# A scan and gated feed-forward kernel: its head reordered, small work moved to GpSimd, weight loads moved

## The chip, the cores and the metric

The kernel runs on one core of one Trainium2 chip. The metric is the time of one execution on the device, in microseconds; of the kernel before there are three runs, whose median is compared. A core has TensorE (PE, with PEld for its weight loads), VectorE (DVE), ScalarE (ACT), GpSimd (POOL) and SyncE (SP), which run side by side, each its own instructions in their order, and wait for each other on semaphores. DMA transfers are issued by SP and ScalarE on hardware queues (q1 and q10 in the profile) and by GpSimd on a software queue (q0), and all of them share 16 DMA engines.

## What is computed

A Mamba-2 style scan over 4 batches, 8 heads and 768 tokens, and a bilinear feed-forward layer on its output. Cut to what matters:

```python
for c in range(nc):                          # chunks of tokens
    cum = np.cumsum(log_a[chunk], axis=-1)
    L = np.exp(cum[:, None] - cum[None, :]) * causal
    M = (Cc @ Bc.T) * L                      # scores, masked and decayed
    y[chunk] = M @ xc + (Cc @ state) * np.exp(cum)
    state = np.exp(cum[-1]) * state + (Bc * np.exp(cum[-1] - cum)).T @ xc
x2 = y.transpose(0, 2, 1, 3).reshape(3072, 256)
out = ((x2 @ w_a) * (x2 @ w_b)) @ w_out      # 256 -> 1536 -> 256
```

Inputs and output are float32. The kernel uses blocks of 128 tokens, six in all, and running products of `a` in place of sums of logarithms.

## The kernel before

Tokens go by blocks of 128 (`NBLK` = 6); a block of all four batches is two pairs of two batches each, so pairs 0 and 1 are block 0, pairs 2 and 3 block 1, and so on. All is written for one core under a schedule given by hand: each engine's instructions stand in the order of the code, and the tile framework only adds the waits. Every transfer stands on its issuer's queue in that order too.

*Loads.* SP and ScalarE load `a` and B and C (`bn`, `cn`) of pairs 0 and 1 (lines 192 to 202). GpSimd loads x of pair 0 (`xn`), half 0 of Wa, x of pair 1, half 0 of Wb and half 1 of Wa (227 to 233), all cast to float16 on the way; half 1 of Wb comes later (812), and the two halves of Wo at 870 and 880. SP's loads of C and B of block 1 (`cq`, `bq`, 813) wait until half 0 of Wa has landed, and x and B of pairs 2 and 3 follow them.

*The chain of a pair in block 0.* VectorE scans `a` to running products (`scan`, 242) and takes the reciprocal at mid block (`over_mid`); TensorE turns the two into per-token factors (`factors_mm`, 257). B and C are scaled by them (`scale_bc`, 318, to `bm` and `cm`), transposed on TensorE (`transposes`, 361) and copied out by VectorE (`bt`) and ScalarE (`ct`). `scores` (392) makes C B^T in four PSUM banks, `mask` (436) multiplies by the causal table, three of four times on VectorE, once by a ScalarE copy `tmp` and a product on GpSimd. The output product (`pv_u`, 445, for pair 0; `pv1`, 516, for pair 1) multiplies by x, and the result is copied to `X2T`, the feed-forward layer's input. `ds_mm` makes the state's contribution.

*The feed-forward layer of block 0.* `unit_mm` (588) makes two of twelve slices of 128 of x2 @ w_a or x2 @ w_b in one bank, four matmuls of 256 columns. `evac_a` (605) copies the first factor to SBUF on ScalarE; `times` (610) multiplies by the second on VectorE, or, with `by_pool`, after another ScalarE copy on GpSimd; `go` (728) runs whole units. `out_mm` (629) multiplies by Wo. The four banks for all this and for the factors go round in the order of the digits of `BANKS` (22), one per `bank()` call.

*Later blocks* take their factors from rows (`mid_rows`, 280; `turned_rows`, 290, a transpose on VectorE to `Pt`; `batch_factors`, 295, four copies to `FC`; `batch_inverse`, 302, their reciprocal `FB`). `scale_q` (335) multiplies C and B by them on GpSimd into `planes`, whose gaps `clear` (286) has set to zero, and `turn` (347) transposes them on VectorE. `state_sums`, `state_spread` and `state_decay` (562 to 587) carry the state, with decay tables `G` and `Ge` (862, 864; `Ge` uses `parS`, 824, which is `par` times a constant).

*Fillers.* `warmup` (235) issues matmuls on zeros that nothing reads, in places where TensorE would else have nothing to do.

The step of this schedule that the change touches is lines 769 to 891. After it TensorE runs the blocks 1 to 5 by the same functions.

Of the kernel before, what the change touches and what calls it, by code (L numbers as in the profile page):

```python
# [19 lines left out]
SS = 64.0  # L20

BANKS = (
    "012313123123123012301230120312301223012301203120312032130210321032130123012301203213021302"
    "1301203120312031201320132013201320132013201320312031203120312031203120312031203120312"
# [4 lines left out]
def kernel(  # L29
# [100 lines left out]
    def bank(name):  # L130
        return psf.tile([128, 512], f32, name=name, tag=f"ff{next(banks)}")
# [84 lines left out]
    )  # L216
    by_row = ident[0:BH, 0:BH].rearrange("p (b g e) -> p b g e", b=nb, e=2)
# [14 lines left out]
    load_w(0, Wb)  # L232
# [69 lines left out]
    def batch_inverse(lo, hi):  # L302
        nc.vector.reciprocal(FB[:, lo:hi], FC[:, lo:hi])
# [284 lines left out]
    def unit_mm(p, k2, W):  # L588
        ps = bank("aps" if W is Wa else "bps")
        for kk in range(2):  # L590
# [178 lines left out]
    warmup(6, SC[3])  # L769
    warmup(2, SC[3], 128)  # L770
# [8 lines left out]
    warmup(1, SC[3], 128)  # L779
# [4 lines left out]
    mid_rows(0, 1, nc.vector)  # L784
# [11 lines left out]
    clear(planes[0], nc.vector)  # L796
# [3 lines left out]
    scale_bc(1, 0, nc.gpsimd)  # L800
# [6 lines left out]
    scale_bc(1, 1, nc.vector)  # L807
    pv_u(0, 1, py, True)
    for bt in range(2):
        evac0(1, bt, (nc.scalar, nc.vector)[bt], py)  # L810
    scan(4, 5)
# [11 lines left out]
    turned_rows(0, 1)  # L823
    nc.vector.tensor_scalar(parS, par, SS, None, ALU.mult)
    scan(5, NBLK)
    over_mid(2, NBLK)
    clear(planes[1], nc.vector)
# [15 lines left out]
    mid_rows(1, NT, nc.gpsimd)  # L843
# [3 lines left out]
    warmup(1, fps[:, 128:512], 384)  # L847
    bps = [unit_mm(0, k2, Wb) for k2 in range(2)]
    gps = fps[:, 96 : 96 + H // 2 * NG]
# [10 lines left out]
    times(0, 0, bps[0], asb[0])  # L860
    pv1()
    nc.scalar.copy(G.rearrange("p g k -> p (g k)"), gps)
    batch_factors(0, 1, *range(nb))
# [6 lines left out]
    load_wo(0)  # L870
    ds_mm(0, SC[0][:, 0:256])
    bps.append(unit_mm(0, 2, Wb))
    for k2 in range(1, 3):
        times(0, k2, bps[k2], asb[k2])
    batch_inverse(0, 1)
    nc.vector.reciprocal(flat(fB, 1, 2), fps[:, 2 * NBP * H : 4 * NBP * H])
    scale_q(2, 1, nc.gpsimd)
    scale_q(3, 1, nc.gpsimd)
    scale_q(2, 0, nc.gpsimd)
    load_wo(1)  # L880
    scale_q(3, 0, nc.gpsimd)
    go((1, 0), (1, 1), (1, 2))
    state_sums(0)
# [4 lines left out]
    for (p, k2), a_sb_ in zip(late, asb):  # L888
        times(p, k2, unit_mm(p, k2, Wb), a_sb_)
        if k2 == 3 and p == 0:  # L890
            turn(2)
# [171 lines left out]
```

## Time and profile before

| | |
|---|---|
| median of 3 runs | 123.48 us (123.34 to 124.47) |
| the profiled execution | 123.55 us, span 121.8 us |
| busy: TensorE, VectorE, ScalarE, GpSimd | 116.1, 90.4, 67.2, 56.5 us |
| fillers on TensorE (line 237, by their two outputs and the third) | 23 instructions, the last at 12.86 us |
| B of pair 1, asked for by ScalarE | issued 3.60 us, 6.4 us to landing |
| half 0 of Wa, half 0 of Wb, half 1 of Wa, half 1 of Wb | issued 4.05, 6.12, 6.81, 10.72 us; 5.9, 6.6, 8.9, 7.4 us to landing |
| half 0 and half 1 of Wo | issued 16.04, 21.03 us; 7.1, 5.3 us to landing |
| first product of Wo (line 632) | 24.98 us |

The profile is of one execution, by the hardware's own records. Its page gives busy times, the span in 40 slices, the DMA queues, the chain of work that ended last, and the costliest groups of instructions; the trace behind it answers for single instructions, their waits and their transfers. Busy shares are means over the span, and engines wait for different things at different times, so a stage is read by what its last wait was for.

### The profile page before, as it was taken

To read this page: it belongs to the slowest core of one execution; us is meant where nothing else is said; L and a number is where in the kernel's file an instruction comes from. 1 tells how busy PE (TensorE), PEld (TensorE's weight loads), DVE (VectorE), ACT (ScalarE), POOL (GpSimd) and SP (SyncE) were. 2 spreads that over 40 slices of the span, in tenths; PEclk is the share of its full clock that TensorE was granted. 3 is DMA by queue.
4 is the path that set the end of the run, shared out by engine and by line. 5 is a ranking of instruction groups with operands and counts; after the bars stand their busy time and mean duration, and the time that the engine had idled before them with its cause. 6 is when DMAs were issued, how large, how long until landed. Compare 5 with 4: busy or idle time off the path is not lost.

```text
span 121.8 us, 3560 instructions
## 1 busy us (share of the span) xinstructions
PE 116.1 (95%) x1389; PEld 74.2 (61%) x1389; DVE 90.4 (74%) x170; ACT 67.2 (55%) x135; POOL 56.5 (46%) x87
## 2 busy tenths in 40 slices
PE   5989899999999999999999999999999999999990
PEld 2445789788744468644476464766464684655880
DVE  4898987998998995599966989687799435748000
ACT  0435577557767654567666637545645537565220
POOL 7976757789999839395901995200000000000000
PEclk9999999999999999999999999999999999999999
DMA  2999999995969996999952909312001012010132
GB/s 62 135 179 196 221 226 209 143 201 109 101 82 168 113 151 91 100 178 182 223 25 74 97 1 117 21 43 86 5 0 46 11 50 74 0 43 0 43 102 76
DMA packets 59777, 12.13 MB, mean 100 GB/s; under 512 B 54992, under 2 KB 59728, under 8 KB 59760
## 3 DMA queue, kind: packets, MB, share of 16 engines
q0 software_dynamic: 20256, 3.67, 40.8%
q1 hardware_dynamic: 36976, 7.87, 35.9%
q10 hardware_dynamic: 2528, 0.36, 1.8%
q8 instruction: 11, 0.18, 0.6%
q14 instruction: 6, 0.05, 0.1%
HBM read 12.42 MB, written 3.15 MB: 128 GB/s over the span
## 4 chain that ended last, share of the span: by engine, by line
PE 84%; DMA 5%; DVE 4%; ACTq 2%; issue 1%; POOL 1%; ACT 0%; POOLq 0%; DVEq 0%
PE ops L688 22%; PE aps L662 22%; PE bps L662 21%; DMA bn<-in_B_dram 5%; PE ops L632 4%; PE SC L398 3%; PE aps L593 3%; PE bps L593 3%; ACTq L154 2%; PE SC L467 2%; DVE t L443 1%; PE SC L531 1%; DVE hk L617 1%; PE SC L479 1%; DVE bt L379 1%
## 5 line engine op out<-in xcount | busy, mean ns | idle before, releaser
L607 ACT COPY asb<-aps 128x512 f32<-128x512 f32 x72 | 41.9, 586 | 17.1 <-PE aps L662 13.4
L674 DVE TENSOR_TENSOR hkb<-bps,asb 128x512 f16<-128x512 f32 x60 | 40.3, 686 | 12.0 <-ACT asb L607 10.7
L662 PE MATMUL aps<-XB,Wa 128*128 128x512 f16 x120 | 35.8, 379 | 0.0
L662 PE MATMUL bps<-XB,Wb 128*128 128x512 f16 x120 | 35.7, 379 | 0.0
L688 PE MATMUL ops<-Wo,hkb 128*128 128x256 f16 (+1 forms) x252 | 28.1, 268 | 0.0
L688 PEld LDWEIGHTS <-hkb 128*128 128x128 f16 x252 | 23.0, 98 | 3.8
L662 PEld LDWEIGHTS <-Wb 128*128 128x128 f16 x120 | 12.4, 103 | 13.5
L662 PEld LDWEIGHTS <-Wa 128*128 128x128 f16 x120 | 12.1, 103 | 11.7 <-issue 0.5
L443 DVE TENSOR_TENSOR t<-SC,causal_q 128x512 f16<-128x512 f32 x27 | 17.3, 681 | 2.4 <-PE SC L398 2.4
L700 ACT ACTIVATE osb<-ops 128x256 f32<-128x256 f32 (+1 forms) x20 | 7.6, 378 | 18.4 <-PE ops L688 18.4
L441 POOL TENSOR_TENSOR t<-tmp,causal_q 128x512 f16<-128x512 f32 x5 | 5.8, 1156 | 11.4 <-ACT tmp L440 11.4
L176 POOL DMA_DIRECT2D xn<-in_x_dram x8 | 9.6, 1200 | 0.0
L340 POOL TENSOR_TENSOR planes<-cq,FC 128x256 f16<-128x256 f32 x10 | 7.6, 772 | 2.3 <-DMA x<-in_x_dram 2.2
L617 DVE TENSOR_TENSOR hk<-bps,asb 128x512 f16<-128x512 f32 x12 | 7.8, 671 | 1.1 <-PE bps L593 0.6
L340 POOL TENSOR_TENSOR planes<-bq,FB 128x256 f16<-128x256 f32 x10 | 7.7, 774 | 0.1
L443 DVE TENSOR_TENSOR t<-SC,causal 128x512 f16<-128x512 f32 x11 | 6.9, 671 | 0.5 <-PE SC L398 0.5
L553 ACT ACTIVATE XB<-SC 128x512 f16<-128x512 f32 (+1 forms) x10 | 5.1, 552 | 4.0 <-PE SC L495 2.4
L440 ACT COPY tmp<-SC 128x512 f32<-128x512 f32 x10 | 5.9, 588 | 2.2 <-PE SC L398 1.8
L593 PE MATMUL aps<-X2T,Wa 128*128 128x256 f16 x48 | 6.7, 273 | 0.2 <-DVE hk L617 0.2
L593 PE MATMUL bps<-X2T,Wb 128*128 128x256 f16 x48 | 6.8, 273 | 0.0
L441 POOL TENSOR_TENSOR t<-tmp,causal 128x512 f16<-128x512 f32 x5 | 5.8, 1152 | 2.1 <-ACT tmp L440 1.9
L237 PE MATMUL SC<-warm 128*128 128x512 f16 (+1 forms) x15 | 4.9, 473 | 1.3 <-DVE warm L204 1.3
(102 smaller groups left out, 107.2 us busy)
## 6 DMA issues: line engine op xcount, KB each, us to landing
out_dram<-osb SPq DMA_DIRECT2D x23, 128.0 KB, 1.8
cq<-in_C_dram SPq DMA_DIRECT2D x20, 64.0 KB, 4.2
bq<-in_B_dram SPq DMA_DIRECT2D x20, 64.0 KB, 3.8
bn<-in_B_dram SPq DMA_DIRECT2D x8, 128.0 KB, 4.1
xn<-in_x_dram POOLq DMA_DIRECT2D x8, 128.0 KB, 5.6
Wa<-in_moe_w_a_dram POOLq DMA_DIRECT2D x2, 384.0 KB, 7.4
Wb<-in_moe_w_b_dram POOLq DMA_DIRECT2D x2, 384.0 KB, 7.0
Wo<-in_moe_w_out_dram POOLq DMA_DIRECT2D x2, 384.0 KB, 6.2
```

Of the source, the lines that this page charges most:

```text
L176: eng.dma_start(by_token(pair_in[p][which]).rearrange("p t h n -> p (t h) n"), src.rearrange("t h q n -> q (t h) n"))
L340: eng.tensor_tensor(out=plane[:, c0 : c0 + 4 * step].rearrange("p (j c) s -> p j s c", c=step)[:, :, :, 0:N], in0=by_batch[blk][which][:, ...
L440: nc.scalar.copy(tmp, i_)
L441: nc.gpsimd.tensor_tensor(out=o_, in0=tmp, in1=c_, op=ALU.mult)
L443: nc.vector.tensor_tensor(out=o_, in0=i_, in1=c_, op=ALU.mult)
L593: nc.tensor.matmul(ps[:, kk * 2 * Q : (kk + 1) * 2 * Q], W[k // 6][:, f, k % 6 // 3 * 384 : (k % 6 // 3 + 1) * 384].rearrange("p (c kk) -> ...
L607: (nc.vector.tensor_copy if on_dve else nc.scalar.copy)(asb, a_ps)
L617: eng.tensor_tensor(out=s["hk"][:, 2 * k2 : 2 * k2 + 2, :].rearrange("p k q -> p (k q)"), in0=b_ps, in1=asb, op=ALU.mult)
L662: nc.tensor.matmul(t_, W[k // 6][:, f, k % 6 // 3 * 384 : (k % 6 // 3 + 1) * 384].rearrange("p (c kk) -> p kk c", kk=3)[:, k % 3], XB[:, b ...
L674: return lambda: nc.vector.tensor_tensor(out=s["hk"][:, k], in0=ps[1], in1=asb, op=ALU.mult)
L688: nc.tensor.matmul(o_ps[:, 0:w], hk[:, k, c * Q : (c + 1) * Q], Wo[:, k, cs], start=(k == 0), stop=(k == NK - 1), skip_group_check=True,)
L700: nc.scalar.activation(out=o_sb[:, 0:w], in_=o_ps[:, 0:w], func=AF.Copy, scale=1.0 / (YS * YS))
```

## The change

It rewrites the order of the head and of block 0's feed-forward units. Cut to its core:

```diff
@@ tables, behind the reduction to par
+    nc.vector.tensor_scalar(parS, par, SS, None, ALU.mult)
@@ first loads, by GpSimd
         if p == 0:
             w0 = load_w(0, Wa)
-    load_w(0, Wb)
+            load_w(0, Wb)
     load_w(1, Wa)
@@
-    def unit_mm(p, k2, W):
-        ps = bank("aps" if W is Wa else "bps")
-        for kk in range(2):
+    def unit_mm(p, k2, W, ps=None, kks=(0, 1)):
+        if ps is None:
+            ps = bank("aps" if W is Wa else "bps")
+        for kk in kks:
@@ pair 0
-    warmup(6, SC[3])
-    warmup(2, SC[3], 128)
+    warmup(5, SC[3])
+    warmup(1, SC[3], 128)
...
     warmup(2, SC[3])
-    warmup(1, SC[3], 128)
...
-    mid_rows(0, 1, nc.vector)
+    mid_rows(0, 1, nc.gpsimd)
...
-    clear(planes[0], nc.vector)
+    clear(planes[0], nc.gpsimd)
     warmup(1, tcp)
     factors_mm(1, 2, fps, 1)
     warmup(2, tcp)
-    scale_bc(1, 0, nc.gpsimd)
...
     scale_bc(1, 1, nc.vector)
+    scan(4, 5)
+    scale_bc(1, 0, nc.vector)
+    clear(planes[1], nc.gpsimd)
     pv_u(0, 1, py, True)
     for bt in range(2):
         evac0(1, bt, (nc.scalar, nc.vector)[bt], py)
-    scan(4, 5)
     load_w(1, Wb)
@@ pair 1
     transposes(1, apart=True)
     aps = [unit_mm(0, 0, Wa)]
-    turned_rows(0, 1)
-    nc.vector.tensor_scalar(parS, par, SS, None, ALU.mult)
     scan(5, NBLK)
     over_mid(2, NBLK)
-    clear(planes[1], nc.vector)
     clear(planes[2], nc.gpsimd)
...
     mask(product(1, 3), by_pool=True)
-    mid_rows(1, NT, nc.gpsimd)
     asb.append(evac_a(aps[2]))
     for m in range(3):
         mask(product(1, m))
-    warmup(1, fps[:, 128:512], 384)
     bps = [unit_mm(0, k2, Wb) for k2 in range(2)]
+    bps.append(unit_mm(0, 2, Wb, kks=(0,)))
...
     times(0, 0, bps[0], asb[0])
+    times(0, 1, bps[1], asb[1], by_pool=True)
     pv1()
+    ds_mm(0, SC[0][:, 0:256])
+    unit_mm(0, 2, Wb, bps[2], (1,))
     nc.scalar.copy(G.rearrange("p g k -> p (g k)"), gps)
-    batch_factors(0, 1, *range(nb))
-    nc.gpsimd.tensor_tensor(
-        out=Ge.rearrange("p k (g e) -> p g k e", e=2),
-        in0=G.unsqueeze(3).broadcast_to((128, H // 2, NG, 2)),
-        in1=parS.unsqueeze(1).unsqueeze(1).broadcast_to((128, H // 2, NG, 2)),
-        op=ALU.mult,
-    )
-    load_wo(0)
-    ds_mm(0, SC[0][:, 0:256])
-    bps.append(unit_mm(0, 2, Wb))
-    for k2 in range(1, 3):
-        times(0, k2, bps[k2], asb[k2])
+    times(0, 2, bps[2], asb[2])
+    turned_rows(0, 1)
+    mid_rows(1, NT, nc.gpsimd)
+    batch_factors(0, 1, *range(nb), eng=nc.gpsimd)
+    load_wo(0)
+    go((1, 0))
     batch_inverse(0, 1)
+    go((1, 1))
     nc.vector.reciprocal(flat(fB, 1, 2), fps[:, 2 * NBP * H : 4 * NBP * H])
+    go((1, 2))
     scale_q(2, 1, nc.gpsimd)
     scale_q(3, 1, nc.gpsimd)
     scale_q(2, 0, nc.gpsimd)
     load_wo(1)
     scale_q(3, 0, nc.gpsimd)
-    go((1, 0), (1, 1), (1, 2))
     state_sums(0)
+    nc.gpsimd.tensor_tensor(
+        out=Ge.rearrange("p k (g e) -> p g k e", e=2),
+        in0=G.unsqueeze(3).broadcast_to((128, H // 2, NG, 2)),
+        in1=parS.unsqueeze(1).unsqueeze(1).broadcast_to((128, H // 2, NG, 2)),
+        op=ALU.mult,
+    )
     spread(0)
...
-        if k2 == 3 and p == 0:
+        if k2 == 4:
             turn(2)
```

The digits of `BANKS` change with it, so the feed-forward units of the whole kernel go round the four banks in another order. In the new order the bank of Wb unit (1, 1), which `times` on VectorE frees, is the one that Wa unit (0, 3) takes; before, it took that of Wa unit (1, 1), which ScalarE's copy frees. The instructions that compute are otherwise the same: TensorE has one product of 512, two of 128 and one of 384 columns less, all of them fillers, and ScalarE copies one bank more for GpSimd in place of four small copies.

## The prediction

> **What bounds the kernel now.** I read the page's slices first, to see which engine is full and when, then the chain of waits from the start to 16 us, then TensorE's timeline for its own waits, then busy time by stretch, and last the DMA queues around the end of the chain's long transfer.
>
> The slices (tenths of each fortieth of the span, 3.05 us):
> ```profile
> PE   5989899999999999999999999999999999999990
> ```
> TensorE is full from the fifth slice to the end. Only the head, some 15 us, holds time that a new order can give back. The chain of waits (start us, us, what) says what paces it:
> ```profile
> 3.60 6.44 DMA bn<-in_B_dram
> ...
> 10.16 0.63 POOL bm L327
> ...
> 10.84 0.41 PE SC L368 x4
> ...
> 11.27 0.69 DVE bt L379
> 11.96 0.31 DVE Pt L291
> 12.27 0.05 DVE parS L824
> 12.32 0.34 DVE Pr L244
> ...
> 12.82 0.17 DVE planes L288
> 12.99 1.75 DVE t L443 x3
> ```
> B of pair 1, asked for at 3.60, lands at 10.04; call L = 10.07 the moment it counts. From there GpSimd scales it, TensorE transposes, VectorE copies out, then does five small things (transpose, parS, scan, reciprocal, clear) and the masks, and only then can the output product of pair 1 (L452) start, at 14.78, L + 4.71. What TensorE does meanwhile, from its timeline:
> ```profile
> 12.86 0.33 PE L237 MATMUL fps<-warm 128*128 128x384 f16 x1
> 14.78 0.42 PE L452 MATMUL SC<-t,xn 64*32 64x128 f16 x32 [0.40 <-DVE t L443]
> 22.54 0.60 PE L593 MATMUL aps<-X2T,Wa 128*128 128x256 f16 x4 [0.17 <-DVE hk L617]
> ```
> One filler product and one wait of 0.40, then a wait of 0.17 at 22.54, the last in the span that the waits list gives TensorE. By stretch (us; busy PE, PEld, DVE, ACT, POOL; clock; DMA):
> ```profile
> 10.07:14.78 4.71, 4.17 (x76) 2.98 (x62) 4.20 (x12) 2.77 (x6) 3.23 (x8) 1.00 1.19 216
> 14.78:22.50 7.72, 7.60 (x124) 6.80 (x124) 6.64 (x14) 5.04 (x13) 5.39 (x10) 1.00 1.23 207
> ```
> VectorE leaves 0.5 of 4.71 and 1.08 of 7.72 idle. After 22.5 the chain holds TensorE's work alone, which the change keeps, so the end moves by what TensorE has gained when it reaches the scores of pair 2 (23.1).
>
> **The sum's base.** The profiled execution took 123.55, of which 121.8 is the span and 1.75 lies around it; the median of three is 123.48, 0.07 less.
>
> **Scaling B of pair 1 on VectorE.** Before: 0.09 issue + 0.63 on GpSimd + 0.05 = L + 0.77 for the transposes. VectorE did the same shape for pair 0 in 0.42 (L327), so L + 0.56. VectorE must be free at L. It ended pair 0's masks at 9.55; ahead of B now stand cm (0.36) and a scan (0.41), which alone would end at 10.32. But mid_rows (0.27) leaves VectorE ahead of pair 0's bt, which followed it without idle time, and clear (0.17) leaves too; fewer fillers ahead of the first factors let these start when selr is done (3.85) and not at 4.15. Some 0.25 to 0.5 earlier: free at 9.8 to 10.05. If neither reaches the masks, 0.25 of the gain is lost.
>
> **X2T behind it.** The copy-out of output 0's last quarter (0.29) now stands behind bm: done at L + 0.77, so the first Wa products start at L + 0.83 (before L + 1.00); eight take 0.97, and the scores start at L + 1.80 (before L + 1.97).
>
> **The small steps taken out.** Pair 0 shows 7.09 to 7.66 from scores to masks, 0.57. So masks at L + 2.37, if VectorE is free: bt starts 0.43 after the transposes (10.84 to 11.27), L + 0.99, ends L + 1.68, scan 0.34 and reciprocal with its gaps 0.16 end L + 2.18. Before, masks stood at L + 2.92. They end at L + 4.12. The fourth mask is GpSimd's: ScalarE's ct (0.39), two copies (1.07), tmp (0.60) and gaps end about L + 3.1, plus 1.14 is L + 4.25, which is later and decides: the product's second part starts 0.46 earlier than L + 4.71. TensorE's list fits: from L + 2.2 one Wa unit 0.44, ten Wb products 1.1, the G product 0.39 end at L + 4.1; the filler (0.33) is gone. Half of the third Wb unit, two of four products, 0.22, now lies ahead of the output product: that is 0.22 less behind it. So far 0.68.
>
> **Edits that other work hides.** parS (0.12) goes into VectorE's wait of 0.77 for the first transfer; without that cover it would delay the first scan by as much. mid_rows of block 1 (by its row of 512 columns, 1.03, about 0.3) goes into GpSimd's wait of 0.82 ahead of its first mask, two clears (0.23 each) into the wait of 0.62 that bm leaves with it; what is queued behind them, the issue of Wb's second half, still comes sooner than at 10.72, and the planes they clear are first written at 18.96. Uncovered they would cost 0.8 in all. SP's queue keeps its order: C of block 1 waits for the first Wa, as before. turned_rows (0.39) moves behind the masks, into VectorE's wait between two bilinear products.
>
> **GpSimd's new work.** One product of the bilinear stage goes over ScalarE (0.58) to GpSimd (its masks, same size, take 1.15), which frees VectorE of 0.64. GpSimd then does this product (to L + 5.4), mid_rows (1.03, L + 6.45) and four FC copies of 32x32. No row has them there: ScalarE does one in 0.216, GpSimd one three times as wide in 0.259, a memset of one column in 0.10; between 0.10 and 0.26 I take 0.2, nearest to the copies. They end at L + 7.25. The reciprocal FB (0.34) waits for them, with a bilinear product (0.63) queued behind it on VectorE, and that product frees the bank of Wa unit (0,3): L + 8.3. TensorE would reach it at L + 4.25 + 4.10 - 0.22 = L + 8.13 (4.10 from 14.78 to 18.88). A new wait of 0.2, between none and 0.4 with the copies' ends. The wait of 0.17 at 22.54 goes, as VectorE has 0.64 less and turn(2) stands one product later; GpSimd's scale_q for it waits for C of block 1 at 18.96, as before, and ends near 21.2, when VectorE still has products to do. Sum: 0.68 - 0.2 + 0.17 = 0.65.
>
> **Wb ahead of x of pair 1.** Wb lands at 6.12 + 6.6 = 12.7, and its first product is at 13.02; with TensorE earlier it would be the next to be late, so its move is needed and otherwise worth nothing. x of pair 1 (landing 10.2 to 11.4) then comes behind 384 KB, 1.9 us at 207 GB/s: 13.3, still ahead of L + 4.16 = 14.2. What it may cost is L itself. Two answers of the DMA view, 7.5 to 9.0 and 9.0 to 9.5:
> ```profile
> q0 software_dynamic: 244, 0.29, 111.7%
> q10 hardware_dynamic: 66, 0.01, 5.8%
> ...
> q0 software_dynamic: 416, 0.08, 188.7%
> q10 hardware_dynamic: 21, 0.00, 4.6%
> ```
> q10 carries B of pair 1. It passed 44 packets/us beside Wa and 42/us beside x: what q0 moves seemed not to matter, cost zero. From the other side: q0's packets took 0.036 us each while they were x (554 in 9.5 to 10.1 at 209.8% of 16 engines) and 0.111 each while mostly weights (464 in 10.1 to 12.8 at 119.5%). If each of the last 21 packets of B lets one of q0 past, Wb adds 0.075 for each that shares an engine: 0.3 over five engines, 1.6 on one. No gain: the swap changes only what follows Wa on q0. I take 0.1, near the measured rates. The Trainium skill, in DMA: Bandwidth & Descriptors, Queues, rings and completion order, says that each DMA engine goes round its queues a packet at a time; it speaks against this move, and by it the sum would be 0.35 rather than 0.55; the two rates above don't bear it out.
>
> **Wo later.** It was issued at 16.04 and landed at 23.1, used at 24.98. GpSimd now comes to it at about 17.3: landing between 23.1 (if the queue is its limit; Wb's second half lands only at 18.1) and 24.4. It is used at 24.4. Taken as nothing; at worst it eats 0.3. What it leaves free on the engines may bring C of block 1 sooner, which nothing waits for but GpSimd. The later Ge and scale_q keep their cover: spair is read at 29.03.
>
> Forecast: 0.65 - 0.1 = 0.55 gained, 123.55 - 0.55 - 0.07, some 122.95, say 123.0.
>
> **Rivals.** *The gain is given back* on new waits: FB 0.4 for 0.2, Wo 0.3, or B 0.3: 0.55 - 0.2 - 0.3 is about nothing, 123.2 to 123.7. For it: VectorE is busy 6.64 of 7.72 there, and four separate links must each hold. Against: it loses 0.64. *B pushed back, slower*: all the late packets share one or two engines; 1.6 or 0.8 later, less 0.65, is 123.6 to 124.5; it decides from 0.65 on. For it: q10 had passed 406 packets in the microsecond from 6.5, before Wa filled q0, and then 44/us, so q0 paces it. *The clock rises late, slower*: the fillers of 512 columns take 606 to 634 ns until 5.5 and 379 to 390 from 6.1 on, though the clock row shows full throughout. Now TensorE, out of fillers, idles some 0.3 before the first factors. If the rise came after L, the 22 Wa and Wb products ahead of pair 1's output would take some 0.1 more each, 1.3 to 2.2, net 0.7 to 1.6: 124.2 to 125.1. Against: 0.46 of idle time at 6.6 did not undo it. The Trainium skill, in TensorE: Matmul & The Clock Gate, Part 1, has the clock doubled after one busy window of about 3.4 us; that the trace agrees (1.26 to 6.1 busy) is all that it shows, not how much idling a window stands. *More than forecast*: no new wait and all of TensorE's idle time and filler back (0.54 + 0.12 + 0.33 + 0.22): 122.3.
>
> **How the numbers follow.** Forecast 0.48 (122.6 to 123.2), given back 0.27, B pushed back 0.09, late clock 0.07, more 0.09. The range 122.4 to 124.0 leaves out the low half of the last and the high parts of the slower two, about 0.15. One per cent (1.23 us) is what a measurement tells from no change: faster than 122.25 needs the best case and some luck, 0.06; over 124.7, the high ends of B and clock, 0.08; the rest 0.86.
>
> **What would show it.** bm on VectorE within 0.1 of B's landing, B landing before 10.2; L452 starting 0.4 to 0.5 earlier; no filler and no wait over 0.15 before it; FB waiting for GpSimd's FC; scores of pair 2 near 22.5; fillers at 380 ns by 6.5. Wrong if B lands after 10.7, if L632 waits for Wo, or if TensorE waits over 0.5 in all between 15 and 25.

## The result and the profile after

The changed kernel takes 125.14 us (median of 14 runs, 124.05 to 125.82), the kernel before 123.54 (14 runs, 123.34 to 125.36): a ratio of 1.0119, 95% interval [1.0091, 1.0147]. It is 1.6 us slower, where 0.5 faster was forecast. Disturbed runs are left out of the ratios, which are not the quotients of these medians. The profiled execution of the changed kernel took 124.05, with a span of 122.3; it is the fastest of the 14. So there are two things to explain: why even this one is 0.5 behind the profiled execution of before (123.55), and why most executions are a further microsecond behind it.

TensorE's row of the page's slices is as full as before from the seventh slice on (the sixth, 15.3 to 18.3 us, has an 8 for a 9), and tells little:
```profile
PE   5999889999999999999999999999999999999990
```
The chain of waits of the changed kernel (start us, us, what), from the transposes of pair 1 to Wa unit (0, 3) and the two behind it:
```profile
10.52 0.28 PE SC L369 x4
10.80 0.87 PE aps L595 x8
11.67 0.36 PE SC L399 x32
...
14.11 0.42 PE SC L453 x32
14.53 0.32 PE SC L507 x27
14.84 0.92 issue
15.76 0.23 PE SC L507 x4
15.99 0.35 PE bps L595 x2
16.43 0.69 DVE hk L619
17.12 0.31 DVE Pt L292
...
18.21 0.21 POOL FC L298
...
18.72 0.64 DVE hk L619
19.40 1.47 PE aps L595 x12
```
The first four lines are the head as forecast. B and GpSimd have left the chain, and TensorE is its own limit up to the output product of pair 1 (L453), which starts at 14.11 and not at 14.78: 0.67 earlier. Then comes a stretch that the kernel before did not have, 0.92 of "issue", a wait for nothing that the profile shows: of the 32 products of L507, 16 of `ds_mm(1)` in `pv1` and then 16 of `ds_mm(0)`, 28 are done, and the last four start only at 15.76. From there the chain goes through VectorE and GpSimd and back to TensorE at 19.40.

TensorE's timeline gives its waits (start us, us, engine, line, operation, in brackets the idle time ahead and what ended it):
```profile
3.90 0.61 PE L266 MATMUL fps<-selr,Pr 32*64 32x16 f32 x8 [0.21 <-DVE selr L251]
15.76 0.23 PE L507 MATMUL SC<-xn,bm 64*32 64x64 f16 x4 [0.92 <-issue]
19.40 1.47 PE L595 MATMUL aps<-X2T,Wa 128*128 128x256 f16 x12 [0.16 <-DVE hk L619]
```
The wait of 0.17 at 22.54 is gone, as forecast; the wait for `hk` at Wa unit (0, 3) has come, as forecast; the 0.92 is new; and there is 0.21 at 3.90, ahead of the first factors.

By stretch, cut at the output product (us; busy PE, PEld, DVE, ACT, POOL; clock; DMA):
```profile
9.95:14.11 4.16, 4.13 (x69) 3.05 (x63) 3.71 (x10) 3.35 (x7) 2.36 (x6) 1.00 1.41 198
14.11:22.30 8.19, 7.11 (x117) 6.18 (x117) 5.54 (x12) 3.77 (x8) 6.87 (x12) 1.00 0.99 167
```
Up to 14.11 TensorE idles for 0.03. In the next stretch it idles for 1.08 (0.12 before), VectorE for 2.65 (1.08 before), and GpSimd is busy 6.87 of 8.19. TensorE's 1.08 are the 0.92 of "issue" and the 0.16 for `hk`; GpSimd, the fullest of the others, is what stands behind the second.

Setting the starts of the same instruction side by side, counted back from the last (the output product by its own name, as the order around it is new), gives a ledger against the profiled execution of before (minus is earlier). Two later versions, with the fillers back, stand beside it; they are explained below.

| TensorE reaches | before, us | changed | a_fill_pad | a_first_wb_wait |
|---|---|---|---|---|
| output product of pair 1 | 14.78 | -0.67 | -0.53 | -0.51 |
| Wb unit of pair 1 | 16.61 | +0.20 | -0.69 | -0.67 |
| next Wa unit | 17.84 | +0.37 | -0.53 | -0.50 |
| Wa unit (0, 3) | 18.72 | +0.69 | -0.12 | -0.42 |
| Wa unit behind the old wait | 22.54 | +0.35 | -0.45 | -0.75 |
| block 1's state product (L506 before) | 30.17 | +0.30 | -0.11 | -0.29 |
| Wb unit of block 1 | 34.60 | +0.53 | +0.16 | -0.24 |

### The profile page after: what moved, and what is told of

It reads as the page before. It is cut to its first block, busy times and chain, and to the rows that moved or that the text cites. A ratio compares the mean times of both kernels' runs of the same rounds, so it can differ in the third digit from the quotient of the medians.

```text
span 122.3 us, 3552 instructions
## 1 busy us (share of the span) xinstructions
PE 116.5 (95%) x1385; PEld 74.1 (61%) x1385; DVE 89.9 (74%) x167; ACT 67.1 (55%) x132; POOL 58.5 (48%) x94
## 4 chain that ended last, share of the span: by engine, by line
PE 90%; DVE 3%; DMA 2%; issue 1%; ACT 1%; POOL 1%; DVEq 0%
PE ops L690 22%; PE aps L664 21%; PE bps L664 21%; PE ops L634 4%; PE SC L399 4%; PE bps L595 3%; PE aps L595 3%; PE SC L468 2%; DMA a_sb<-in_a_dram 2%; PE tc L238 2%; PE SC L238 1%; DVE hk L619 1%; PE SC L532 1%; PE fps L266 1%; POOL FC L298 1%
## 5 line engine op out<-in xcount | busy, mean ns | idle before, releaser
L619 DVE TENSOR_TENSOR hk<-bps,asb 128x512 f16<-128x512 f32 x11 | 7.2, 666 | 2.4 <-PE bps L595 2.3
```

What stands on the lines that cost most here:

```text
L619: eng.tensor_tensor(out=s["hk"][:, 2 * k2 : 2 * k2 + 2, :].rearrange("p k q -> p (k q)"), in0=b_ps, in1=asb, op=ALU.mult)
```

## The experiments

Names that begin with b_ are the kernel before with one part of the change, or without one of its fillers; names with a_ are the changed kernel with a part undone. Each was measured beside the kernel before on its chip, whose medians were 123.54 to 123.78.

| run | us, median | ratio to before, 95% |
|---|---|---|
| a_again (one execution) | 124.38 | |
| a_x_first | 125.36 | 1.014 [1.0111, 1.0169] |
| b_wb_first | 123.68 | 1.0004 [0.9987, 1.0021] |
| a_ds_late | 125.25 | 1.0125 [1.0094, 1.0156] |
| b_nofill | 124.87 | 1.0088 [1.0058, 1.0118] |
| a_fill | 124.13 | 1.0044 [1.002, 1.0069] |
| a_fill_ds | 124.33 | 1.0041 [1.0019, 1.0063] |
| a_fill_pad | 124.06 | 1.004 [1.0013, 1.0067] |
| b_wb1_early | 123.77 | 1.0049 [1.0012, 1.0086] |
| a_pad_rows | 123.86 | 1.0031 [1.0013, 1.005] |
| a_pad_rows_wb | 124.18 | 1.0043 [1.0018, 1.0069] |
| a_pad_rows_wb_fc | 123.48 | 0.9985 [0.9958, 1.0013] |
| b_idle_ahead | 124.66 | 1.005 [1.0017, 1.0083] |
| b_idle_behind | 123.82 | 1.0018 [0.9987, 1.0049] |
| a_best_fc_first | 124.41 | 1.0044 [1.0017, 1.0071] |
| a_head_only | 124.04 | 1.0012 [0.9982, 1.0041] |
| a_first_wb_wait | 123.30 | 0.9969 [0.9931, 1.0006] |
| a_fc_wb_wait | 123.20 | 0.9963 [0.9936, 0.9991] |

The theories after the result, by the letters that the expectations use: F, TensorE's instructions come too late; D, the data of `ds_mm(0)` come too late; V, the new waits of VectorE and GpSimd; O, the order of Wb and x; C, the clock; later Q, half 1 of Wb stands ahead of C of block 1 on the DMA engines; S, ScalarE's own instructions come late.

### A second execution, and the order of Wb and x

a_again is the changed kernel once more.

> The changed kernel as it is, for a second trace. Theory F (fetch): TensorE stands still in the middle of ds_mm(0), 28 of 32 matmuls done, because its next 16 KB of instructions have not come; these come by the queue q8, whose 11 packets of 16384 bytes are what 2,770 instructions of TensorE take. Then the hole is at the same instruction again (the 449th row of TensorE with its weight loads) within a few, its length varies with the transfers, 0.9 to 2.5 us, and the run's time above 123.1 varies with it. Theory D (data): something that ds_mm(0) reads is late; then the hole is at the same place too, but ends with a landing or another engine's end. Theory V (new waits on VectorE and GpSimd: FB behind FC, the bank of Wa unit (0,3)) has the loss between 16 and 23 us, and no hole is needed.

It took 124.38. The stretch of "issue" is there again, 0.85 at the same product, so it is not an accident of one execution.

a_x_first puts x of pair 1 back ahead of Wb; b_wb_first makes the reverse edit, the swap alone, in the kernel before:
```diff
         if p == 0:
             w0 = load_w(0, Wa)
-            load_w(0, Wb)
+    load_w(0, Wb)
     load_w(1, Wa)
```

> The changed kernel with x of pair 1 ahead of the first half of Wb again. Theory O (order): Wb ahead of x holds up q8's packet or x itself, and is the loss; then the hole of 0.9 us or more goes and the time falls to 123.0 to 123.5. Theory F: the packet is late because TensorE comes sooner and the 16 DMA engines are full whichever of the two is first; then q8's first packet still starts after 13.0, the hole stays within 0.5 us of the changed kernel's, and the time stays at 124.3 to 125.5. By the prediction's step on Wb, its first product would also wait some 0.3, as Wb lands near 12.7.

> The kernel before with the first half of Wb ahead of x of pair 1 and nothing else. Theory O: 0.5 to 1.5 us slower than before, 124.0 to 125.0, with a hole of TensorE near 15 us. Theory F: q8's first packet starts at 12.8 to 13.4, TensorE comes to the same instruction at 15.5 and finds it or waits at most 0.3; 123.4 to 123.8. If B of pair 1 lands later behind Wb, as the prediction feared, it shows here as a later POOL bm (before 10.16).

The swap alone costs and brings nothing (1.0004), and in b_wb_first GpSimd starts on B of pair 1 at 9.67, not later than before. Theory O falls, and with it the rival that had B pushed back. a_x_first is slower than the profiled executions of the changed kernel, but not by the order: in its execution six fillers took 616 ns each, where 386 is their time in the kernel before. That led to the clock.

### The clock: three fillers fewer

```diff
-    warmup(6, SC[3])
-    warmup(2, SC[3], 128)
+    warmup(5, SC[3])
+    warmup(1, SC[3], 128)
...
     warmup(2, SC[3])
-    warmup(1, SC[3], 128)
```
b_nofill takes these three out of the kernel before and changes nothing else; a_fill puts them back into the changed kernel. b_idle_ahead takes out the two ahead of the first factors alone, b_idle_behind the one behind them alone.

> The kernel before with the change's three edits to the fillers ahead of pair 0's products and nothing else: one of 512 columns and two of 128 fewer. Theory C (clock): TensorE's clock rises only after it has been kept busy without a gap; with the fillers gone it stands 0.2 to 0.3 us before the first factors, and in most executions the rise comes at 7.4 to 12.7 us in place of 5.0 to 6.1. Then this kernel alone shows it: the fillers of 512 columns still take 606 to 634 ns after 7 us, and the time is 124.0 to 125.2, scattered over more than 1 us. Theory F (fetch of instructions) and theory V (new waits on VectorE and GpSimd): nothing of the loss is here, 123.3 to 123.8.

> The changed kernel with those three fillers put back and nothing else. Theory C: the clock rises by 6.5 us in each execution, the scores of pair 1 start by 11.7, and the time falls from 125.1 to at most 124.3 with a scatter as small as before's. Theory F: what is left over 123.0 is the hole of 0.8 to 0.9 us in ds_mm(0), which this kernel still shows, now 8 rows of instructions earlier in the program: 123.7 to 124.3. Without F no hole and 122.9 to 123.2. Theory V: 125.

> The kernel before without the fillers of 512 and of 128 columns that stand ahead of the first factors (the third filler that the change takes out stays). Theory C1: TensorE's idle time of 0.2 at 3.9, ahead of the factors, lets the clock rise late in most executions, as the late-clock rival of the prediction has it: 124.5 to 125.0, as without all three (124.87). Rival C2: what counts is TensorE's idle time behind the first factors, where the third filler stood: 123.4 to 123.7, the head being no later than before.

> The kernel before without the filler of 128 columns behind the first factors alone. Theory C1: nothing idles ahead of the factors and the clock rises as before: 123.4 to 123.7. Rival C2: 124.5 to 125.0. If both this run and the one without the fillers ahead stay under 124.0, it takes both idle times together.

Taken out of the kernel before, the three cost 1.3 us in the median (123.57 to 124.87). Put back into the changed kernel they bring 1.0 (125.14 to 124.13). The two ahead of the factors do it: 124.66 without them beside 123.78, and 123.82 without the third alone. The groups of TensorE between 4.4 and 14 us (count | busy us, mean ns of one | idle) show why. First the fillers on `tc` of the kernel before:
```profile
L237 PE MATMUL tc<-warm 128*128 128x512 f16 x6 | 2.0, 386 | 0.0
```
Then the same six of b_idle_ahead:
```profile
L237 PE MATMUL tc<-warm 128*128 128x512 f16 x6 | 3.3, 616 | 0.0
```
Same instruction, same data, 1.6 times as long: the clock, which in the kernel before has risen by 6.1, rises in this execution only after all six, the last of which starts at 11.21. By the steps between Wa's products behind them, 0.21 us until 12.7 and 0.11 from 12.88 on, it rises at some 12.8. TensorE's timeline of b_idle_ahead shows the one idle stretch that is new, and what it comes to:
```profile
3.88 0.61 PE L265 MATMUL fps<-selr,Pr 32*64 32x16 f32 x8 [0.20 <-DVE selr L250]
...
12.06 1.42 PE L593 MATMUL aps<-X2T,Wa 128*128 128x256 f16 x8
...
15.91 0.42 PE L452 MATMUL SC<-t,xn 64*32 64x128 f16 x32 [0.17 <-DVE t L443]
```
An idle 0.20 us at 3.68 makes the output product of pair 1 start at 15.91, 1.13 later than before, and from there to the end every instruction is 1.14 later. The head is not paced by B any more but by a slow TensorE. The changed kernel has the same idle stretch (0.21 ahead of 3.90). Its profiled execution is one in which the clock rose later than before but still in time, the fillers taking 422 on average: the first, at 7.30, took 606, the second, at 8.20, took 389. In a_x_first and a_ds_late, which have the same fillers, it was 616 again and the output product started at 15.82 and 15.63. The lot differs by execution: b_nofill was measured from 123.64 to 125.56, and its profiled execution, at 123.67, had 386. Over all the traces: in the 14 in which TensorE goes into the first factors without idling, the six fillers take 386; of the six in which it idles there, for 0.06 to 0.22, the clock has risen by 5.7 in one (b_nofill, 0.06), rises between 7.2 and 8.2 in two and between 12.3 and 12.9 in three.

The page's own row of the clock reads full in every slice of all these kernels and is no help here; the duration of a filler of 512 columns is. The Trainium skill, in TensorE: Matmul & The Clock Gate, Part 1, says that the clock is released by one busy window of some 3.4 us, and that the windows run freely, whatever the kernel does; the lot from execution to execution agrees with that. That one busy window is enough does not come out here: in b_idle_ahead TensorE idles for only 0.04 between 3.88 and the rise at some 12.8, which is more than two such windows, so why the rise comes that late stays open. Under "HAM oscillation" it gives as the rule that no idle gap be over 3.4 us. That is a rule for keeping the clock; for getting it, these runs show that 0.2 us can be too much.

### The hole in the output product's tail

a_ds_late moves `ds_mm(0)` behind pair 1's three units; a_fill_ds is that with the fillers back. a_fill_pad has the fillers back and issues those on `SC[3]` in pieces of 128 columns, which is the same work as in a_fill in 54 more instruction rows of TensorE (27 products, each with its weight load).
```diff
-    ds_mm(0, SC[0][:, 0:256])
     unit_mm(0, 2, Wb, bps[2], (1,))
...
     go((1, 2))
+    ds_mm(0, SC[0][:, 0:256])
```
```diff
     def warmup(n, bank, cols=512):
+        if bank is SC[3]:
+            n, cols = n * cols // 128, 128
         for _ in range(n):
```

> The changed kernel with ds_mm(0), 16 small matmuls and 16 weight loads, moved from before the second half of the third Wb unit to after unit (1,2). Theory F: what counts is the number of instructions, so the hole moves with the count, to 28 instructions further on among the large products of units (1,0) and (1,1), where 28 rows take 1.5 us instead of 0.3; TensorE reaches that place 1.2 us later and the hole is 0 to 0.5 us; time 123.2 to 124.2. Theory D: ds_mm(0) takes its wait with it or the wait falls behind other work; no hole at all, and none elsewhere. Theory V: no change from 125.1, as the waits on FC and on the bank are untouched.

> The changed kernel with the three fillers back and ds_mm(0) moved behind unit (1,2). With the clock risen early, theory F: the hole falls 20 to 28 rows further on among large products, TensorE is there at about 15.7 and the instructions at about 15.8: at most 0.3 of hole, and 0.5 less than a_fill, 123.2 to 123.7. Theory D (ds_mm(0) waits for data): no hole, 123.0 to 123.4, and if there is a hole it is in front of ds_mm(0) in its new place.

> The changed kernel with the three fillers back, and the fillers up to pair 0's scores issued as four pieces of 128 columns in place of one of 512: the same columns, 54 rows of instructions more ahead of everything. Theory F: TensorE's stream is cut into pieces by count, so the piece that was late ends 62 rows earlier in the program than in the changed kernel, at the start of pair 1's ds_mm, and is asked for earlier, among pair 0's products; the hole in ds_mm(0) goes or is at the new place and under 0.4: 123.0 to 123.6. Theory D: the hole stays in ds_mm(0), 0.8 to 0.9, 123.7 to 124.3.

a_ds_late could not tell: its clock rose late, the output product came at 15.63, and nothing waited. a_fill had no hole either, since in its execution B of pair 1 landed late (10.87) and the product came at 15.09. The other two tell D from F. In a_fill_ds `ds_mm(0)` is elsewhere and the product at that place of TensorE's list, the 224th, is one of a large unit, which nothing holds; in a_fill_pad `ds_mm(0)` stands where the change put it, and it runs through, at 14.50:
```profile
14.25 0.42 PE L455 MATMUL SC<-t,xn 64*32 64x128 f16 x32
14.50 0.55 PE L509 MATMUL SC<-xn,bm 64*32 64x64 f16 x32
14.98 0.40 PE L597 MATMUL bps<-X2T,Wb 128*128 128x256 f16 x2
```
The kernel before ran through them too:
```profile
15.03 0.54 PE L506 MATMUL SC<-xn,bm 64*32 64x64 f16 x32
```
The data are the same and earlier than ever, so D falls. What moved is the place in TensorE's instructions. The queue q8, of the kind "instruction", carries 11 packets of 16384 bytes in the span, and in all four traces in which TensorE stopped here, it stopped ahead of its 224th product (the 448th row, with the weight loads), whichever of the 32 that was, and started it 1.37 to 1.55 us after the first of the packets had ended:

| | first q8 packet ends | 224th product starts | which of the 32 | idle ahead of it |
|---|---|---|---|---|
| before | 13.74 | 15.32 | 27th | 0 |
| b_wb_first | 13.87 | 15.24 | 27th | 0.06 |
| b_nofill | 13.94 | 15.49 | 30th | 0.18 "issue" |
| changed | 14.31 | 15.76 | 29th | 0.92 "issue" |
| a_again | 14.36 | 15.75 | 29th | 0.85 "issue" |

By this the kernel before, whose product started 1.58 after its packet, reached it about when it could start. The change was ready for it 0.64 earlier (the product ahead of it starts at 14.65, 15.29 before), but its packet ended 0.57 later, and the product started 0.44 later than before. In a_fill_pad, with more rows ahead, the first packet ends at 11.44 and no product waits. F stands as far as this goes; why the packet comes when it comes was not tried. Nor does any pair of runs show what the hole costs in the median: a_fill, of whose executions only the profiled one is known to be without it, and a_fill_pad lie at 1.0044 and 1.004. Where the clock rises late there is no hole, since TensorE then comes late itself (a_x_first, a_ds_late): the two losses do not add up in one execution. The Trainium skill, in Runtime: NRT & Kernel Launch, Instruction fetch mechanics, says that instructions are refilled in blocks of 16 KiB and that crossing a block is mostly hidden. The packet size agrees; here it is not hidden, among 32 products of 64 columns that take 0.5 us together.

Yet a_fill_pad, without a hole, is at 124.06. The ledger says where its 0.69 went: 0.57 by Wa unit (0, 3), 0.34 in block 1 and 0.27 by 34.60, against 0.33 that the wait gone at 22.54 gives. Each loss has a group below.

### The product and the small copies on GpSimd

a_pad_rows is a_fill_pad with VectorE's `turned_rows(0, 1)` ahead of `times(0, 2)`.

> The changed kernel with the three fillers back, the fillers on SC[3] in pieces of 128 columns (124.06 so far), and VectorE's turned_rows of block 1 put ahead of its third product times(0, 2), not behind it. Theory V (the wait for FB): GpSimd's FC copies waited 1.07 us for Pt, and FB and two bilinear products of VectorE stood behind them, which cost TensorE 0.3 to 0.4 at Wa unit (0, 3). Then Pt is done some 0.6 earlier, FC with it, FB before 18.1, and TensorE's wait for hk at Wa unit (0, 3) falls below 0.15; about 0.3 is gained there, and the time is 123.7 to 123.9. Rival: VectorE is what is full there, so that turned_rows only puts 0.39 in front of times(0, 2), the wait for hk stays over 0.25 and the time stays 124.0 to 124.2.

Pt is done 1.0 earlier (15.50, 16.48 in a_fill_pad) and FC starts when it did, at 16.69. GpSimd's timeline of a_pad_rows:
```profile
14.47 1.27 POOL L621 TENSOR_TENSOR hk<-asb 128x512 f16<-128x512 f32 x1 [0.57 <-ACT asb L611]
15.70 1.03 POOL L285 TENSOR_TENSOR Ps<-Pr,rmid 32x512 f32<-32x512 f32 x1
16.69 0.94 POOL L300 COPY FC<-Pt 32x32 f32<-32x32 f32 x4
```
Nothing waits between the three: FC's way is GpSimd's own, the product, the rows and four copies of 0.23. The 0.16 of the ledger at 17.84 is not FC's: there TensorE waits for VectorE's product at 16.58, and that for ScalarE's copy `asb`. TensorE's wait at Wa unit (0, 3) stays at 0.25, as the rival has it; its ratio, 1.0031, and that of a_fill_pad, 1.004, lie within each other's intervals.

a_best_fc_first is meant to take that away: FC ahead of the rows on GpSimd (it also issues half 1 of Wb a little later, and gives ScalarE four idle copies, both for the groups below).
```diff
-    mid_rows(1, NT, nc.gpsimd)
     batch_factors(0, 1, *range(nb), eng=nc.gpsimd)
+    mid_rows(1, NT, nc.gpsimd)
...
     nc.vector.memset(zero, 0.0)
+    for i in range(4):
+        nc.scalar.copy(spare[:, i : i + 1], zero[:, 0:1])
```

> The changed kernel with fillers back, fillers on SC[3] in pieces, turned_rows earlier and half 1 of Wb later (124.18, its profiled execution 123.22), and two things more: GpSimd makes its four FC copies ahead of mid_rows of the later blocks, not behind, and ScalarE runs four copies of one column at the start that nothing reads, so that it has 245 instructions as in the kernel before. Theory V: FC waited for GpSimd's own work; now FC ends near 16.7, FB before 17.2, and TensorE's wait for hk at Wa unit (0, 3) (0.25) is under 0.1. Theory S: the gap of 0.39 ahead of ScalarE's copy asb at 33 us is 0.06 as in all kernels with 244 or 245 of its instructions. Together 0.5: 123.2 to 123.5, and less than before where the clock rises early (span 121.1 or less). Rival: neither the order nor the number counts; wait and gap stay, and the time is 123.9 to 124.3.

FC ran at 15.94 to 16.88, FB at 17.43, and TensorE no longer waits at Wa unit (0, 3): V is shown for that wait. The time, 124.41, is another matter, below.

Two runs undo the part instead. a_pad_rows_wb_fc gives FC back to ScalarE (`batch_factors(0, 1, *range(nb))`), and a_head_only gives VectorE the second bilinear product back as well (`times(0, 1, ...)` without `by_pool`, behind `pv1()`), so that of the change only the head, Wb ahead of x and the later Wo and Ge are left.

> As the run with half 1 of Wb later, and the four FC copies are ScalarE's again, as in the kernel before: this takes the part 'small copies by GpSimd' out of the change. ScalarE then runs one instruction more than before and not three less. Theory S (ScalarE's own instruction supply): in all kernels with the change, ScalarE's copy asb of block 1's first feed-forward unit started 0.39 us after what released it, in all without it 0.06; if that comes from the number of instructions ahead of it, the gap is 0.1 or less here and Wb's unit near 34.6 comes 0.2 to 0.3 sooner: 123.0 to 123.3. Rival: the gap stays 0.3 or more, since it comes from the data, and the time is within 0.15 of the run with half 1 of Wb later, or worse by what four copies of 0.22 on ScalarE cost.

> The version that gave 123.48 (FC copies back on ScalarE, half 1 of Wb later, turned_rows earlier, fillers back and in pieces), with the second bilinear product back on VectorE too, behind the output copy of pair 1, so that of the change only the head's order, Wb ahead of x and the later Wo and Ge are left. If the product on GpSimd is worth VectorE's 0.64, the wait for VectorE's hk at 22.5 (0.17) comes back and the time is 123.4 to 123.8. Rival: ScalarE is what is full once it has FC (its copy for GpSimd, 0.58, stands ahead of asb, and TensorE waited 0.27 for that), so the time falls: 122.9 to 123.3.

The first came to 123.48, level with the kernel before, the second to 124.04, level too (1.0012). The gain of the head is spent in both by 17.84: in a_head_only the output product starts at 14.09, but VectorE's product now stands ahead of the one that frees a bank (TensorE waits 0.47 for `hk` at 15.68), and ScalarE's four FC copies, 0.90, stand ahead of `asb` (0.35 at 17.52); the ledger reads -0.26, then +0.40. In a_pad_rows_wb_fc 0.73 goes already ahead of the output product, which starts at 14.73: TensorE's first products of Wb wait until 13.21, 0.05 after half 0 of Wb has landed, which was at 11.58 in the changed kernel and is at 13.16 here. So either engine, given the work back, holds TensorE, and neither of the two expectations for a_head_only, 123.4 to 123.8 and 122.9 to 123.3, holds.

### Half 1 of Wb ahead of C of block 1

In every a_ kernel so far GpSimd's `bm` of pair 2 in block 1 waits for B, 0.6 to 2.4 us, and in some of them `bm`, or `mask` queued behind it, then holds TensorE in block 1: it loses 0.34 there in a_fill_pad and 0.28 in a_again. In the profiled execution of the changed kernel `bm` waits 0.62 and TensorE loses nothing, so this is no part of its 0.5. B comes late because x, ahead of it on SP's queue, is issued late, and that waits for C. b_wb1_early makes only this in the kernel before: GpSimd asks for half 1 of Wb before its product for pair 1.
```diff
+    load_w(1, Wb)
     scale_bc(1, 0, nc.gpsimd)
...
     scan(4, 5)
-    load_w(1, Wb)
```

> The kernel before, with one thing changed: GpSimd asks for half 1 of Wb ahead of its product bm of B of pair 1, not behind it. Theory Q (the queue): in the changed kernel SP's loads of x for pairs 2 and 3 come late (issued 16.6 to 17.8 us against 15.9 to 16.8 where bm is GpSimd's) because half 1 of Wb, issued 1.1 us earlier, puts 384 KB more in front of C of block 1. Then here C's transfer takes 6.7 us or more (6.0 before), x is issued after 16.5, and GpSimd waits over 0.4 for B of pair 2. bm itself starts some 0.2 later behind the 0.76 of the issue. Time 123.8 to 124.1. Rival R (x is late from something else that the change does): C takes 6.0 to 6.4 us, x is issued before 16.4, and only the 0.2 of bm shows: 123.6 to 123.8.

SP's queue in b_wb1_early (start us, us, what, count):
```profile
10.71 1.80 SPq L162 DMA_DIRECT2D cq<-in_C_dram  x4
12.56 2.92 SPq L162 DMA_DIRECT2D bq<-in_B_dram  x4
17.92 2.55 SPq L154 DMA_DIRECT2D x<-in_x_dram  x3
```
And GpSimd at `bm` of pair 2:
```profile
28.19 0.62 POOL L327 TENSOR_TENSOR bm<-bn,fB 128x256 f16<-128x256 f32 x1 [1.01 <-DMA bn<-in_B_dram]
```
From C's issue to x's issue it is 7.2 us (6.0 in the kernel before, 9.93 to 15.89), B is waited for 1.01 (no wait before), TensorE loses 0.25 in block 1, where `ds_mm` waits for `bm`, besides 0.13 in the head, and the median is 0.23 up. Q is shown in this direction. a_pad_rows_wb was to show the other.

> As the run with turned_rows earlier, and GpSimd asks for half 1 of Wb behind its clear of the third plane, some 0.9 us later than in the changed kernel, about where the kernel before had it. Theory Q: C of block 1 takes 6.0 to 6.4 us again, x is issued before 16.4, GpSimd waits less than 0.3 for B of pair 2, and of the 0.4 to 0.6 that the changed kernel loses in block 1 (23 to 30 us) more than half comes back: 123.3 to 123.6. Rival R: x stays after 16.6, nothing comes back, and the time is as in the run with turned_rows alone.

Its edit did not do what it says: behind `clear(planes[2])` the load was issued at 9.71, where it had been 9.43, still ahead of C (9.85). It took 124.18, though its profiled execution, at 123.22 the fastest of its ten, lost nothing in block 1. a_best_fc_first has the same place, 9.70, 0.69 ahead of C, and the worst of it: B of pair 2 waited for 2.43, and 1.4 us gone at once at the output of block 1. So the last two runs make the load wait for VectorE's last `X2T` copy of pair 0, at 10.5, as late as in the kernel before:
```diff
-    load_w(1, Wb)
+    tc.add_manual_dep(load_w(1, Wb).ins, x2t.ins.name, AFTER, ...)
```
a_first_wb_wait is a_best_fc_first with this, a_fc_wb_wait is a_pad_rows_wb_fc with this.

> The version with FC on GpSimd ahead of mid_rows and four idle ScalarE copies (124.41), with one thing changed: GpSimd's load of half 1 of Wb waits for VectorE's last X2T copy of pair 0, so that it is issued at 10.5 to 10.7 us, as in the kernel before, and not at 9.70. Theory Q: C of block 1, issued at 9.7 to 10.4, then takes 6.0 to 6.5 us (7.1 in that version), x is issued before 16.8, GpSimd waits under 0.5 for B of pair 2 (2.43 there), and the time is 123.2 to 123.7. Rival R: C's time comes from when Wa's half 0 and B of pair 1 land, or from the chip: C takes 6.7 us or more all the same and the time stays at 124.1 to 124.6.

> The version with FC on ScalarE and the second bilinear product on GpSimd (123.48), with the same wait ahead of the load of half 1 of Wb. Theory Q: C 6.0 to 6.5 us, x issued before 16.8, B of pair 2 waited for under 0.5 (0.85 there): 123.1 to 123.4. Rival R: C takes 6.7 us or more and the time is 123.4 to 123.8.

Issued at 10.82 and 10.87, 0.6 to 0.7 behind C, it lets C pass: x is issued 5.0 and 5.9 us after C. SP's queue of a_first_wb_wait:
```profile
10.15 2.81 SPq L163 DMA_DIRECT2D cq<-in_C_dram  x4
13.01 1.93 SPq L163 DMA_DIRECT2D bq<-in_B_dram  x4
15.17 5.12 SPq L155 DMA_DIRECT2D x<-in_x_dram  x4
```
The median falls from 124.41 to 123.30, and from 123.48 to 123.20; the first pair of intervals lies apart, the second overlaps. In a_first_wb_wait B of pair 2 is still waited for 1.21, for a reason that the runs don't show, but the wait ends at 27.52 and not at 28.96; in a_fc_wb_wait `bm` starts at 27.01 with no wait. Over all kernels of this study the interval from C's issue to x's goes with the order: 5.0 to 6.0 where half 1 of Wb is issued behind C (before, b_nofill and these two; 6.7 in b_idle_behind, only 0.12 behind), 6.4 to 7.6 where it is ahead. The Trainium skill, in DMA: Bandwidth & Descriptors, Queues, rings and completion order, has each engine go round its queues a packet at a time. The longer interval fits that, and so does the swap of Wb and x, which stand on one queue and cost nothing; that the sharing is by packets no run here shows.

a_fc_wb_wait is 0.4% faster than the kernel before, [0.9936, 0.9991]. a_first_wb_wait has the fastest executions of all (five of 12 from 122.66 to 122.86, where the kernel before beside it had none below 123.28), but others up to 124.45; in its profiled execution, 123.30, TensorE is 0.75 ahead at 22.54. Both still wait for half 0 of Wb ahead of the output product, 0.19 in a_first_wb_wait and 0.47 in a_fc_wb_wait, where it starts at 14.61.

### ScalarE at 33 us

Of the last 0.27 of the ledger, by 34.60, 0.23 come from one copy of ScalarE (0.04 from block 1), and so do 0.23 in the changed kernel. Its timeline in the changed kernel:
```profile
32.94 0.39 ACT L646 ACTIVATE osb<-ops 128x256 f32<-128x256 f32 x1 [0.27 <-PE ops L634]
33.77 1.11 ACT L609 COPY asb<-aps 128x512 f32<-128x512 f32 x2 [0.44 <-PE bps L664]
```
In a_first_wb_wait:
```profile
32.40 0.39 ACT L651 ACTIVATE osb<-ops 128x256 f32<-128x256 f32 x1 [0.27 <-PE ops L639]
32.89 0.59 ACT L614 COPY asb<-aps 128x512 f32<-128x512 f32 x1
```
In the changed kernel the copy starts 0.43 after the end of its product, in the other 0.09, as in the kernel before (from the release, as the expectations count, 0.39 and 0.06). It is 0.42 or 0.43 in all nine kernels with 241 ScalarE instructions in the trace, where it is the 64th of them, and 0.09 in all eleven with 244 or 245, where it is the 67th or 68th, be the difference the FC copies or four copies that nothing reads. That is S's forecast, and 20 kernels agree that the number decides, though no run changes it alone: a_best_fc_first moves FC as well. That ScalarE's own refill is what falls there is argued from TensorE's case and not shown. The other queue of the kind "instruction", q14, speaks against a wait for a packet: in the nine kernels one of its packets ends 0.84 to 1.23 us ahead of the copy, and the gap is the same in all.

## Why the prediction was wrong

- *The head.* Right in mechanism and nearly in size. VectorE is free for `bm` at 9.95 (9.8 to 10.05 forecast), and from there to the output product it takes 4.16 (4.25 forecast). That the product comes 0.67 earlier and not 0.46 is 0.09 by this and 0.12 by luck: B had landed at 9.77, 0.27 earlier than before, so that `bm` need not wait until 10.07. In a_fill, with B at 10.87, the product came at 15.09. With 0.22 of Wb's unit ahead of it besides, as forecast, 0.69 is in hand at 16.61 in a_fill_pad, where neither clock nor hole interferes.
- *Fewer fillers let the factors start at 3.85 and not at 4.15.* They did, at 3.90, and it was booked as a gain. This step failed. It opened the idle 0.2 that lets the clock rise late, and is worth some 1.0 us of the 1.6: the rival that was given a chance of 0.07, with its price, 1.3 to 2.2 before the gain is taken off, somewhat high (1.3 in b_nofill, 1.0 from the changed kernel to a_fill). The argument against it, that 0.46 of idle time at 6.6 did no harm, took a wait that stands behind the rise for one that stands ahead of it. b_idle_ahead shows what one ahead of it does; b_idle_behind, which opens none ahead of the rise, costs nothing. The sign that the prediction itself named, fillers at 380 ns by 6.5, failed even in the profiled execution: 631 at 5.95 and 606 at 7.30.
- *What TensorE does meanwhile.* The sum took it that TensorE runs an instruction as soon as its data are there. At 14.84 it had none: 0.87 of the gain went at once. No row of before showed a wait of this kind, but the 224th product started there 1.58 after q8's packet ended, and the four that waited 1.37 to 1.55: at most 0.2 to spare.
- *FB behind FC.* Right mechanism, mis-sized: 0.2 forecast, 0.41 lost at Wa unit (0, 3) in a_fill_pad, besides the 0.16 ahead of it that are not FB's. Part of it is a misreading: Wa unit (0, 3) starts at 18.72 and not at 18.88, 3.94 behind the output product and not 4.10, and with that the same sum gives 0.33. The rest: GpSimd's product starts 0.27 late, for ScalarE's copy, and the four copies take 0.23 each and not 0.2.
- *The issue of Wb's second half "still comes sooner", at no cost.* Wrong in sign: sooner is what cost, 0.23 in the kernel before, and 1.1 from a_best_fc_first to a_first_wb_wait (0.9 by their ratios). The prediction asked what the earlier load would be late for and not what it would stand in front of.
- *Wb ahead of x.* 0.1 forecast, nothing measured. The rival with B pushed back falls. That the move makes Wb early enough holds in the changed kernel (landing at 11.58), but not in a_pad_rows_wb_fc and a_fc_wb_wait (13.16 and 13.03).
- *Wo later, parS, the wait at 22.54.* As forecast; `out_mm` started at 25.33 without a wait.
- *The range.* It ended at 124.0 and so left out the late clock, for which the prediction had 124.2 to 125.1. The costs were weighed one by one as rivals; the late clock, FB and ScalarE's copy came together in one kernel, and the hole where the clock is early.

## What to carry to other kernels

Before taking out a filler, look whether TensorE's clock has risen by then, by the duration of one fixed matmul, and in several executions: one idle stretch of 0.2 us ahead of the rise cost some 1 us in most executions, and one of 0.46 behind it left the clock up. When a change lets a load be issued sooner, name what on the other queues it will now stand in front of, and hold it back by a dependency if that is needed first. A gain at one place is only worth what the next stages can take: here 0.69 was in hand at 16.61, and GpSimd's queue, a load and a late copy of ScalarE took it back one after another.

## What the runs showed of the hardware

TensorE's clock rose by 6.1 us or only at some 12.8 in kernels that differ by 0.2 us of idle time at 3.7 (before, b_idle_ahead); 386 against 616 ns for a product of 512 columns. TensorE stopped for 0.85 to 0.92 us at its 224th product in two executions, and for 0.06 and 0.18 at the same count but other products in two more kernels, each time 1.37 to 1.55 us behind the end of a 16384-byte packet of queue q8, and 54 more rows ahead of it made the stop vanish. ScalarE started one copy 0.43 us behind its product with 241 instructions, and 0.09 behind it with 244 or 245, whatever the added ones were.
